# Background convolution of a gated-convolution and MLP kernel: products, fold and butterfly formed on VectorE instead of GpSimd

## The chip, the cores and the metric

The kernel runs on one core of one Trainium2 chip. The metric is the device time of one execution in microseconds. Before the change it is 2691.79 us, the median of three runs (2687.0 to 2693.62). The profile comes from one more execution, of 2694.62 us, whose instructions span 2692.4 us.

## The reference

Two layers, each of a gated long convolution A and an MLP B, act on x of 2048 tokens by 1024 channels, with residuals (layernorm without weights, written `ln`):

```
def _A_ref(q, k, v, shift_k, ssm_k, ssm_D):
    k_shift = sum over t < 4 of k_pad[:, t:t + S] * shift_k[:, 3 - t]
    kv = k_shift * v
    y = irfft(rfft(kv, 2 * S) * rfft(ssm_k, 2 * S))[:S]     # long causal convolution per channel
    return q * (y + kv * ssm_D)

def _B_ref(x, w1, b1, w2, b2):
    r = max(x @ w1 + b1, 0)
    return (r * r) @ w2 + b2

x = A_q
x = x + A(ln(x), A_k, A_v, ...);  x = x + B(ln(x), ...)
x = x + A(ln(x), A_k, A_v, ...);  x = x + B(ln(x), ...)
```

The convolved signal kv does not depend on x, so the result y of the long convolution is the same in both layers and is computed once.

## The kernel before, in words

All engines work from lists that are written out when the program is made; each engine takes its own list strictly in order. The 2048 tokens are cut into four blocks of 512 (`T`). The MLP of one block in one layer is a unit, and `ORDER` lists seven units (the last one takes two blocks together). TensorE multiplies in float32r with every operand split into a high and a low part, three matmuls for one (`mm3`, L351 to L354). A weight tile is loaded into `wr` (L1067, L1070), its high part is cast on ScalarE (`w_hi`, L1080) and its low part, weight minus high part, is formed on VectorE (`w_lo`, L1088; in a few phases on GpSimd). Tiles for three steps ahead are split before a step's matmuls. VectorE also forms the low part of the squared activations (L1565), and takes finished sums of the second matmul out of PSUM (L1685). So TensorE's next step waits for VectorE's list whenever that list is late.

The long convolution runs in the background of these units. Block 0 is done in a first stage of its own (`first_block`, with a planner). For blocks 1 to 3 (`sb`):

- `fwd_x` and `fwd_g` transform 256-token pieces of the signal and of the filter and store them in DRAM, in three versions of each, so that one complex product is made of three real ones (`PAIRS`). VectorE does most of their elementwise work (L382, L384, L424, L461, L481 to L501).
- `prod_stream` loads the transformed pieces into `cx` and `cg` (L642). For output piece j of a channel group and version it multiplies pieces 0 to j of one with pieces j to 0 of the other (`mult`, L542) and sums over the pieces (`red`, L546). Here j runs from 2 to 7. The product has 128 x (j + 1) elements per partition and is stored in `cp` (three buffers) with the j + 1 terms of one sum next to each other. The multiply itself walks through it term by term, so its reads are dense and its stores go in steps of j + 1 words, which is 3 to 8. The sum then reads `cp` densely.
- After the three versions of a group, `fin` combines them: a fold (L692, 512 elements), and a tick later a butterfly of an add and a subtract (L696, L697, 256 elements each). For block 1 plain matmuls follow, for blocks 2 and 3 a split into high and low part (L578 on VectorE) and matmuls for the way back.

`Later` puts a call a given number of ticks later in the program. A tick of `plag` passes with each product. Products are put between the matmul steps at a fixed rate per step (`pace`), slowly in the 18 steps at the end of a unit. The products of blocks 1 and 2 lie in units 0 to 2, those of block 3 in units 3 and 4 (the first few at the end of unit 2). After that there are none.

Before the change the product is on GpSimd, `red` is on VectorE two ticks later, and fold and butterfly are on GpSimd (`FIN` has a letter for each of the blocks 1 to 3: G is GpSimd, V is VectorE).

Of the kernel before, what the change touches and what calls it, by code (L numbers as in the profile page):

```python
# [44 lines left out]
NORM_0 = "VA"  # L45
AHEAD_0 = 4
BURST = 1.06
FIN = "GGG"
PACE_SLACK = {1: 74, 3: 10}
PACE_TO = {1: 2}  # L50
PLAIN = 1
# [196 lines left out]
def tile_h3_mlp(ctx: ExitStack, tc: tile.TileContext, q, kT, vT, shk, ssmT, ssmD, w1, b1, w2, b2,  # L248
                fwd_t, pro_t, inv_t, sgn_t, out):
    nc = tc.nc  # L250
    V, A, G, PE, SY = nc.vector, nc.scalar, nc.gpsimd, nc.tensor, nc.sync
# [284 lines left out]
    def prod_stream():  # L536
        lag = plag
        sums, inv = [0, 0], [0, 0]

        def mult(st, xt, gt, j):  # L540
            pr = cv.tile([P, CU, j + 1], F32, name="cp", bufs=3)
            G.tensor_mul(pr.rearrange("p c i -> p i c"), xt[:, 0:j + 1], gt[:, j::-1])  # L542
            st["pr"] = pr

        def red(st, sm, ty, jj):
# [2 lines left out]
        def fin(st, sm, sb, g, k):  # L548
            s = sm.rearrange("p k j c -> p k (j c)")
            E = ENG[FIN[sb - 1]]  # L550
            if k == 0:
# [81 lines left out]
        def load(n):  # L633
            sb, g, ty = units[n]
            nb = BT * sb + BT
            two = nb <= NBL // 2
            if n % 2 == 0 or not two:
                for nm in ("cx", "cg"):
                    share[nm] = cv.tile([P, 2 if two else 1, nb, CU], F32, name=nm, bufs=2)
            got[n] = [share[nm][:, n % 2 if two else 0] for nm in ("cx", "cg")]  # L640
            for t, src in zip(got[n], (XD[PAIRS[ty][0]], GD[PAIRS[ty][1]])):
                SY.dma_start(t, src[g, :, :nb])  # L642
            when[n] = lag.n

        def fill(n):
            sb = units[n][0]
            room = 3 if BT * sb + BT <= NBL // 2 and n % 2 else 2
            for m in range(n + 1, min(n + room + 1, len(units))):
                if m not in when:
                    if (units[m][0], units[m][1] // 2) not in fwd_done or (m > n + 2 and units[m][0] != sb):  # L650
                        return
                    load(m)

        pair = sm = None
        for n, (sb, g, ty) in enumerate(units):
            while n not in when:
                if (sb, g // 2) in fwd_done:
                    load(n)
                else:
                    lag.tick()  # L660
                    yield None
            while lag.n < when[n] + 2:
                lag.tick()
                yield None
            if ty == 0:
                while sums[0] - sums[1] >= 2:
                    lag.tick()
                    yield None
                sums[0] += 1
                sm = cv.tile([P, 3, BT, CU], F32, name="sm", bufs=2)  # L670
                if g % 2 == 0:
                    pair = {}
            for jj in range(BT):
                j = BT * sb + jj
                st = {"pair": pair}
                mult(st, *got[n], j)
                lag.at(2, red, st, sm, ty, jj)
                if jj == BT - 1:
                    if ty == 2:
                        lag.at(3, fin, st, sm, sb, g, 0)  # L680
                    fill(n)
                lag.tick()
                yield (j + 1) * CU * 1e-3
# [865 lines left out]
    lag = slag  # L1549
    xT = first_block()  # L1550
    pds = prod_stream()
    ml = shut.enter_context(tc.tile_pool(name="ml", bufs=1, reuse_waits="tile"))
    def relu2(st, k):
# [770 lines left out]
```

## Time and profile before

| | |
|---|---|
| median of three runs | 2691.79 us |
| profiled execution | 2694.62 us |
| its span | 2692.4 us |
| TensorE busy | 2629.6 us |
| VectorE busy | 2007.0 us |
| ScalarE busy | 1107.6 us |
| GpSimd busy | 1010.4 us |

The profile names the engines PE (TensorE matmuls), PEld (its weight loads), DVE (VectorE), ACT (ScalarE), POOL (GpSimd) and SP (the queue that issues DMAs). Rows name a source line, an operation, the tiles as output<-inputs, and the shape. "x81 | 76.4, 953 | 10.7" means 81 instructions, busy for 76.4 us together, 953 ns each on average, and 10.7 us in which the engine stood idle just ahead of them. A row of a table of windows gives a stretch of time, then the busy time and the count of each engine in it.

### The profile page before, as it was taken

How to read it: one execution, taken by the hardware profiler on the slowest of the kernel's cores; microseconds unless marked ns; L12 is line 12 of the kernel's file. 1: busy time of each engine (PE TensorE's matmuls, PEld its weight loads, DVE VectorE, ACT ScalarE, POOL GpSimd, SP SyncE). 2: the span in 40 equal slices, each digit the busy share in tenths (PEclk: the TensorE clock that was granted, in tenths of full speed). 3: DMA queues.
4: the chain of work that ended last, by engine and by line, in shares of the span. 5: the costliest groups of instructions: out<-in, count | busy, mean ns of one | idle time of the engine just before them, and what ended most of it. 6: DMA issues, size and time to landing. Idle time of an engine off the chain costs nothing.

```text
span 2692.4 us, 36210 instructions
## 1 busy us (share of the span) xinstructions
PE 2629.6 (98%) x12433; PEld 2204.0 (82%) x12433; DVE 2007.0 (75%) x2957; ACT 1107.6 (41%) x1890; POOL 1010.4 (38%) x641
## 2 busy tenths in 40 slices
PE   7999999899999999999999999999999999999999
PEld 6888787788888888888888888888788778888887
DVE  7878888779887878779767765456778787778553
ACT  3444344343434323343233422335444564444342
POOL 2436665156551744417454275000100006646111
PEclk9999999999999999999999999999999999999999
DMA  7799898679988999888987888689889886888653
GB/s 249 258 306 311 294 306 281 237 267 364 350 299 308 315 328 308 274 293 307 342 304 258 301 291 314 202 266 314 302 295 306 285 300 234 276 259 323 230 188 126
DMA packets 380840, 765.52 MB, mean 284 GB/s; under 512 B 44128, under 2 KB 159472, under 8 KB 377584
## 3 DMA queue, kind: packets, MB, share of 16 engines
q1 hardware_dynamic: 380656, 763.20, 82.7%
q8 instruction: 98, 1.61, 0.2%
q14 instruction: 86, 0.70, 0.1%
HBM read 585.85 MB, written 177.21 MB: 283 GB/s over the span
## 4 chain that ended last, share of the span: by engine, by line
PE 76%; DVE 8%; DMA 8%; POOL 2%; issue 2%; ACT 2%; SPq 1%; DVEq 0%; POOLq 0%; ACTq 0%
PE p L353 22%; PE p L352 22%; PE p L354 22%; PE pt L353 2%; PE pt L354 2%; PE pt L352 2%; PE p L1162 2%; DMA wr<-w 2%; DMA whl<-wd_m 1%; DVE whl L1088 1%; DMA cx<-xd 1%; DMA cg<-gd 1%; DVE st L713 1%; DMA yt<-yd 1%; POOL cp L542 1%
## 5 line engine op out<-in xcount | busy, mean ns | idle before, releaser
L542 POOL TENSOR_TENSOR cp<-cx,cg 128x384 f32<-128x384 f32 (+5 forms) x288 | 543.3, 1899 | 571.4 <-DVE sm L546 378.1
L352 PE MATMUL p<-xh,whl 128*128 128x512 f32 (+1 forms) x1504 | 577.7, 384 | 5.5 <-DMA whl<-wd_m 3.2
L354 PE MATMUL p<-xh,whl 128*128 128x512 f32 (+1 forms) x1504 | 573.5, 381 | 0.6 <-POOL whl L1088 0.6
L353 PE MATMUL p<-xl,whl 128*128 128x512 f32 (+1 forms) x1504 | 573.4, 381 | 0.1
L1080 ACT CAST whl<-wr 128x512 fp32r<-128x512 f32 x545 | 331.7, 619 | 477.1 <-PE p L354 270.6
L1088 DVE TENSOR_TENSOR whl<-wr,whl 128x512 fp32r<-128x512 f32 x495 | 427.5, 875 | 130.7 <-ACT whl L1080 130.1
L352 PE MATMUL p<-whl,rh 128*128 128x512 f32 x1204 | 476.0, 395 | 4.9 <-DMA whl<-wd_m 2.6
L353 PE MATMUL p<-whl,rh 128*128 128x512 f32 x1204 | 471.2, 391 | 4.8 <-DVE whl L1088 4.7
L354 PE MATMUL p<-whl,rl 128*128 128x512 f32 x1204 | 470.6, 391 | 0.0
L352 PEld LDWEIGHTS p<-xh,whl 128*128 128x128 f32 x1504 | 284.1, 189 | 60.9 <-issue 2.4
L354 PEld LDWEIGHTS p<-xh,whl 128*128 128x128 f32 x1504 | 283.6, 189 | 55.5 <-POOL whl L1088 0.8
L353 PEld LDWEIGHTS p<-xl,whl 128*128 128x128 f32 x1504 | 283.9, 189 | 52.4 <-DVE xl L1475 0.3
L1565 DVE TENSOR_TENSOR rl<-wr,rh 128x512 fp32r<-128x512 f32 x140 | 142.4, 1017 | 181.5 <-ACT rh L1562 181.1
L352 PEld LDWEIGHTS p<-whl,rh 128*128 128x128 f32 x1204 | 227.3, 189 | 53.8 <-DMA whl<-wd_m 5.2
L353 PEld LDWEIGHTS p<-whl,rh 128*128 128x128 f32 x1204 | 227.3, 189 | 51.5 <-DVE whl L1088 6.4
L354 PEld LDWEIGHTS p<-whl,rl 128*128 128x128 f32 x1204 | 227.1, 189 | 47.7
L546 DVE TENSOR_REDUCE sm<-cp 128x128 f32<-128x384 f32 (+5 forms) x288 | 249.5, 874 | 11.7 <-POOL cp L542 11.7
L1557 ACT ACTIVATE wr<-p,b1t 128x512 f32<-128x512 f32 x138 | 95.2, 690 | 369.8 <-PE p L354 367.2
L1088 POOL TENSOR_TENSOR whl<-wr,whl 128x512 fp32r<-128x512 f32 x50 | 71.5, 1431 | 274.1 <-ACT whl L1080 257.2
L1685 DVE TENSOR_TENSOR acc<-p,acc 128x512 f32<-128x512 f32 x152 | 99.8, 686 | 83.6 <-PE p L354 83.6
L1044 POOL TENSOR_TENSOR sr<-sr 128x512 f32<-128x512 f32 x14 | 19.9, 1420 | 341.3 <-DMA pd<-wr 303.8
L692 POOL TENSOR_TENSOR sm<-sm 128x512 f32<-128x512 f32 x48 | 69.1, 1440 | 131.5 <-DVE sm L546 123.8
(369 smaller groups left out, 4367.0 us busy)
## 6 DMA issues: line engine op xcount, KB each, us to landing
whl<-wd_m SPq DMA_DIRECT2D x323, 512.0 KB, 5.7
wr<-w SPq DMA_DIRECT2D x441, 256.0 KB, 5.6
wd_m<-whl SPq DMA_DIRECT2D x70, 512.0 KB, 6.4
wr<-td SPq DMA_DIRECT2D x112, 256.0 KB, 4.8
cx<-xd SPq DMA_DIRECT2D x48, 512.0 KB, 5.7
cg<-gd SPq DMA_DIRECT2D x48, 512.0 KB, 6.7
tq<-hd SPq DMA_DIRECT2D x24, 1024.0 KB, 7.4
gd<-fg SPq DMA_DIRECT2D x72, 256.0 KB, 5.9
```

Of the source, the lines that this page charges most:

```text
L352: PE.matmul(o, lh, rh, start=start, stop=False)
L353: PE.matmul(o, lh, rl, start=False, stop=False)
L354: PE.matmul(o, ll, rh, start=False, stop=stop)
L542: G.tensor_mul(pr.rearrange("p c i -> p i c"), xt[:, 0:j + 1], gt[:, j::-1])
L546: V.tensor_reduce(sm[:, ty, jj], st["pr"], axis=AX.X, op=OP.add)
L692: E.tensor_add(s[:, 1:3], s[:, 1:3], s[:, 0:1].to_broadcast([P, 2, s.shape[2]]))
L1080: A.copy(t[:, 0], raws[n]["t"])
L1088: ENG[e[n % len(e)]].tensor_sub(t[:, 1], raws[n]["t"], t[:, 0].bitcast(F32))
L1162: PE.matmul(o, lh, r, start=start, stop=stop)
L1557: A.activation(r, st["o"], AF.Relu, bias=b1t[:, st["f"]:st["f"] + 1])
L1565: V.tensor_sub(st["lo"], st["r"]["t"], st["hi"].bitcast(F32))
L1685: V.tensor_add(accs[tt][:, d], o, accs[tt][:, d])
```

## The change

Products, fold and butterfly go to VectorE for all three blocks, and a sum stands one tick behind its product instead of two. Since the tick passes right after the product has been issued, nothing but the steps of `fin` can come between.

```
-FIN = "GGG"
+FIN = "VVV"
...
-            G.tensor_mul(pr.rearrange("p c i -> p i c"), xt[:, 0:j + 1], gt[:, j::-1])
+            V.tensor_mul(pr.rearrange("p c i -> p i c"), xt[:, 0:j + 1], gt[:, j::-1])
...
-                lag.at(2, red, st, sm, ty, jj)
+                lag.at(1, red, st, sm, ty, jj)
```

The lists of TensorE, ScalarE and the DMA queue keep their order; only buffer numbers differ. The piece below is VectorE's list where the first products of block 1 stand, in unit 0; `whl` is a weight tile whose low part is made, `cp` a product, `sm` the sums.

```order
 L1088 TENSOR_TENSOR whl<-wr,whl 128x512
-L546 TENSOR_REDUCE sm<-cp 128x128
-L1088 TENSOR_TENSOR whl<-wr,whl 128x512
-L546 TENSOR_REDUCE sm<-cp 128x128
+L542 TENSOR_TENSOR cp<-cx,cg 128x3x128
+L546 TENSOR_REDUCE sm<-cp 128x128
+L542 TENSOR_TENSOR cp<-cx,cg 128x4x128
+L546 TENSOR_REDUCE sm<-cp 128x128
+L1088 TENSOR_TENSOR whl<-wr,whl 128x512
 L419 TENSOR_TENSOR fy<-pt,fx 128x8x64
```

Where two sums stood around a weight split, two products with their sums now stand in one piece ahead of it. The next piece is VectorE's list before, in a stretch of unit 3 with products of block 3 (7 and 8 pieces); `rl` is the low part of an activation.

```order
L1565 TENSOR_TENSOR rl<-wr,rh 128x512
L546 TENSOR_REDUCE sm<-cp 128x128
L1088 TENSOR_TENSOR whl<-wr,whl 128x512
L1565 TENSOR_TENSOR rl<-wr,rh 128x512
L546 TENSOR_REDUCE sm<-cp 128x128
L1088 TENSOR_TENSOR whl<-wr,whl 128x512
L546 TENSOR_REDUCE sm<-cp 128x128 x2
L578 TENSOR_TENSOR yl<-sm,yh 128x4x64 x2
```

And this is the same stretch of VectorE's list after the change.

```order
L1565 TENSOR_TENSOR rl<-wr,rh 128x512
L542 TENSOR_TENSOR cp<-cx,cg 128x8x128
L692 TENSOR_TENSOR sm<-sm 128x512
L546 TENSOR_REDUCE sm<-cp 128x128
L1088 TENSOR_TENSOR whl<-wr,whl 128x512
L1565 TENSOR_TENSOR rl<-wr,rh 128x512
L542 TENSOR_TENSOR cp<-cx,cg 128x7x128
L696 TENSOR_TENSOR sm<-sm 128x256
L697 TENSOR_TENSOR sm<-sm 128x4x64
L546 TENSOR_REDUCE sm<-cp 128x128
L1088 TENSOR_TENSOR whl<-wr,whl 128x512
```

A product stands ahead of each sum, and the fold and the butterfly, where they fall due, stand between a product and its sum. GpSimd's list loses all of these and keeps its few weight splits and its residual adds.

## The prediction

> **What bounds the kernel now.** I read the page first.
>
> ```profile
> span 2692.4 us, 36210 instructions
> PE 2629.6 (98%) x12433; PEld 2204.0 (82%) x12433; DVE 2007.0 (75%) x2957; ACT 1107.6 (41%) x1890; POOL 1010.4 (38%) x641
> ```
>
> TensorE is busy for all but 62.8 us of the span, so the kernel is bound by it, and a change on other engines can save those 62.8 us at most. It can cost more, if VectorE becomes too slow for TensorE. A mean of 75% doesn't say whether it does; that is read by stretches. Five stretches hold most of the products: block 1 in unit 0, block 2 in units 1 and 2, block 3 in units 3 and 4. The windows show first what each engine does there, then GpSimd's products alone; the last row is the one in which VectorE is fullest.
>
> ```profile
> core 0: us, PE busy (x) PEld busy (x) DVE busy (x) ACT busy (x) POOL busy (x), PEclk, DMA share, GB/s
> 202.00:471.00 269.00, 255.48 (x1187) 213.70 (x1186) 232.02 (x330) 114.25 (x208) 162.75 (x130) 0.98 0.90 298
> 606.00:807.00 201.00, 199.39 (x948) 167.44 (x947) 179.33 (x230) 82.74 (x150) 114.28 (x70) 1.00 0.96 338
> 875.00:1144.00 269.00, 268.84 (x1281) 226.31 (x1280) 213.64 (x265) 92.40 (x168) 144.93 (x84) 1.00 0.90 306
> 1211.00:1346.00 135.00, 135.00 (x640) 113.52 (x639) 113.51 (x133) 43.20 (x78) 82.68 (x41) 1.00 0.91 325
> 1548.00:1682.00 134.00, 134.00 (x604) 111.42 (x603) 81.27 (x86) 32.72 (x57) 84.94 (x45) 1.00 0.84 302
> ...
> 202.00:471.00 269.00, 117.38 (x87) 0.98 0.90 298
> 606.00:807.00 201.00, 88.37 (x46) 1.00 0.96 338
> 875.00:1144.00 269.00, 105.19 (x53) 1.00 0.90 306
> 1211.00:1346.00 135.00, 58.18 (x25) 1.00 0.91 325
> 1548.00:1682.00 134.00, 61.40 (x27) 1.00 0.84 302
> ...
> 605.00:673.00 68.00, 66.39 (x311) 55.27 (x310) 65.80 (x88) 25.66 (x46) 42.58 (x26) 1.00 1.01 361
> ```
>
> I call them A to E. VectorE has 37, 22, 55, 21 and 53 us left in them. GpSimd's products alone take 117, 88, 105, 58 and 61. They must shrink a lot to fit.
>
> **What the change takes off VectorE.** VectorE's busy time holds more than work. Two DVE rows and one POOL row of the timeline:
>
> ```profile
> 738.76 0.68 DVE L1565 TENSOR_TENSOR rl<-wr,rh 128x512 fp32r<-128x512 f32 x1
> 739.36 2.33 DVE L1088 TENSOR_TENSOR whl<-wr,whl 128x512 fp32r<-128x512 f32 x1
> ...
> 738.91 2.24 POOL L542 TENSOR_TENSOR cp<-cx,cg 128x768 f32<-128x768 f32 x1 [2.89 <-DVE sm L546]
> ```
>
> The first subtract started ahead of GpSimd's product and took 0.68 us. The second, of the same size, started under it, and ended 0.54 us after it (741.69 against 741.15): it stood still while GpSimd worked. How much that is shows against rows from 1750 to 2150 us, where GpSimd does next to nothing:
>
> ```profile
> L1088 DVE TENSOR_TENSOR whl<-wr,whl 128x512 fp32r<-128x512 f32 x131 | 86.7, 685 | 10.1 <-ACT whl L1080 9.6
> L1565 DVE TENSOR_TENSOR rl<-wr,rh 128x512 fp32r<-128x512 f32 x6 | 4.2, 693 | 16.9 <-ACT rh L1562 16.9
> L787 DVE SCALAR_TENSOR_TENSOR px<-yt,rs,px 128x512 f32<-128x512 f32 x8 | 6.0, 752 | 0.3
> L1642 DVE TENSOR_TENSOR cp<-yh,cx 128x1024 fp32r<-128x1024 f32 x7 | 8.6, 1222 | 1.0 <-ACT cx L1638 1.0
> ```
>
> Here are the same kinds in A, and then in D:
>
> ```profile
> L1088 DVE TENSOR_TENSOR whl<-wr,whl 128x512 fp32r<-128x512 f32 x81 | 76.4, 953 | 10.7 <-ACT whl L1080 10.6
> L382 DVE SCALAR_TENSOR_TENSOR fx<-fx,shkt 128x512 f32<-128x512 f32 x21 | 22.1, 1051 | 0.5
> L1565 DVE TENSOR_TENSOR rl<-wr,rh 128x512 fp32r<-128x512 f32 x21 | 18.6, 885 | 5.3 <-ACT rh L1562 5.0
> ...
> L1088 DVE TENSOR_TENSOR whl<-wr,whl 128x512 fp32r<-128x512 f32 x11 | 16.0, 1458 | 0.0
> L1565 DVE TENSOR_TENSOR rl<-wr,rh 128x512 fp32r<-128x512 f32 x13 | 13.6, 1047 | 10.4 <-ACT rh L1562 10.4
> L578 DVE TENSOR_TENSOR yl<-sm,yh 128x256 fp32r<-128x256 f32 x8 | 11.0, 1420 | 0.0
> L382 DVE SCALAR_TENSOR_TENSOR fx<-fx,shkt 128x512 f32<-128x512 f32 x6 | 9.5, 1582 | 0.1
> ```
>
> In A the blocked time is 81 x 0.268 + 21 x 0.299 + 21 x 0.192 = 32 us, or 0.20 us for each of GpSimd's 163 us. In D it is 11 x 0.773 + 13 x 0.354 + 8 x 1.0 (a dense 256 takes 0.42, below) + 6 x 0.83 = 26 us, 0.31 for each of 83. Smaller rows come on top in A, so I take 0.28 per us of GpSimd's moved work.
>
> **What it puts on VectorE.** The rows of 685 and 1222 ns give a dense two-input operation 148 ns + 1.05 ns per element (256 elements: 417 ns). The moved operations on GpSimd, over the whole run:
>
> ```profile
> L542 POOL TENSOR_TENSOR cp<-cx,cg 128x1024 f32<-128x1024 f32 x48 | 124.3, 2589 | 133.6 <-DVE sm L546 133.5
> L542 POOL TENSOR_TENSOR cp<-cx,cg 128x384 f32<-128x384 f32 x48 | 59.8, 1246 | 75.2 <-DMA cg<-gd 72.2 <-DVE sm L546 3.0
> L692 POOL TENSOR_TENSOR sm<-sm 128x512 f32<-128x512 f32 x48 | 69.1, 1440 | 131.5 <-DVE sm L546 123.8 <-DMA whl<-wd_m 4.3 <-ACT whl L1080 3.4
> L696 POOL TENSOR_TENSOR sm<-sm 128x256 f32<-128x256 f32 x49 | 46.7, 954 | 4.6 <-DVE sm L692 3.9
> L697 POOL TENSOR_TENSOR sm<-sm 128x256 f32<-128x256 f32 x49 | 42.7, 871 | 3.8
> ```
>
> A product costs GpSimd 440 ns + 2.10 ns per element. Fold and butterfly come once in six products and cost it 3.27 us; their stores are in long runs, so on VectorE they cost 0.68 + 2 x 0.42, less an overlap that the next rows show.
>
> ```profile
> 1766.16 0.68 DVE L1088 TENSOR_TENSOR whl<-wr,whl 128x512 fp32r<-128x512 f32 x1
> 1766.76 0.42 DVE L1599 TENSOR_TENSOR cx<-cx 128x256 f32<-128x256 f32 x1
> 1767.22 0.42 DVE L1600 TENSOR_TENSOR cx<-cx 128x256 f32<-128x256 f32 x1
> ```
>
> An independent operation starts 0.08 us before the last one ends (0.60 after its start of 0.68). One that reads what the last one wrote starts 0.04 us after it. A set of fold and butterfly is thus 0.60 + 2 x 0.34 = 1.28 us. A sum directly behind its product waits, so a product occupies its whole duration and 0.04 more.
>
> The products' own price is the unknown. No VectorE row of this trace stores elements in steps of several words, as L542 does. From below the dense row bounds it: 0.183 us + 1.05 ns per element. From above there is GpSimd's row with these very stores, 2.10 ns per element, though GpSimd may be held up by something else. I take the second rate, since its store pattern is the one that moves: 0.183 us + 2.10 ns, or GpSimd's time less 0.26 us for each product.
>
> [...]
>
> | us | A | B | C | D | E |
> |---|---|---|---|---|---|
> | VectorE before | 232 | 179 | 214 | 114 | 81 |
> | blocked time gone (0.28 x moved GpSimd time) | -46 | -32 | -38 | -20 | -21 |
> | fold, butterfly (products / 6 x 1.28) | +18 | +10 | +12 | +5 | +5 |
> | products, dense stores | +56 | +43 | +51 | +28 | +30 |
> | or products at 2.10 ns | +95 | +76 | +91 | +52 | +54 |
> | VectorE after, dense | 260 | 200 | 239 | 127 | 95 |
> | VectorE after, 2.10 ns | 299 | 234 | 279 | 151 | 120 |
> | length before | 269 | 201 | 269 | 135 | 134 |
>
> (Each column is rounded after its sum.) The dense products are half of what is left when 0.44 us each is taken off GpSimd's time, plus 0.183 us each. VectorE can be filled to 65.8 of 68 us, 0.97, with TensorE nearly full beside it (last window row). Then A needs 299 / 0.97 = 308 us, +39; B 241, +40; C 288, +19; D 155, +20; E fits. Together +118 us. No store of products can move to a quieter place, for their steps are fixed in the program, and after 1690 us there are none. Between the stretches, at the ends of units, products are few.
>
> Two smaller edits. The sum one tick earlier costs only the 0.12 us of start that I have counted. And VectorE now waits itself for the loads of `cx` and `cg`, with weight splits (L1088) and TensorE's matmuls (L352 to L354) queued behind it:
>
> ```profile
> POOL cp L542 <- DMA cg<-gd: 182.0, 43, 14.4
> ...
> DVE sm L546 <- POOL cp L542: 11.7, 16, 1.9
> ```
>
> GpSimd waits 182 us for these loads because it runs ahead. The sums, two ticks on, waited only 11.7 us for load and product together, so I take nothing here, and 12 us or so at worst.
>
> The profiled execution gives 2694.6 + 118 = 2813 us; the median of the runs lies 2.8 us lower, so I predict **2810 us**.
>
> **The rivals.**
>
> *Stores that cost VectorE nothing.* Then only B overflows: 200 / 0.97 = 206, +6 us, 2698 us at the median, which a measurement of this kernel hardly tells from before (0.3% is 8 us). For it speaks that GpSimd's rate may be its reading of two inputs and not its stores; against it, that steps are untested on VectorE. Fuller short windows within a stretch could make it some 20 us more. Chance 0.18.
>
> *Stores that cost VectorE more than GpSimd.* At a fifth more per element A to D need 324, 255, 304 and 165 us and E still fits: +175 us, 2867 us. GpSimd's slow pace would then have hidden a slower store. It decides as soon as the elements cost over 2.3 ns. Chance 0.18. [...]
>
> *Faster, as single long blocks did the harm.* TensorE's worst wait for VectorE in A is for one of its transform steps:
>
> ```profile
> PE pt L437 <- DVE fx L384: 9.2, 3, 6.7
> ```
>
> If such waits came from single blocks of over 2 us and not from load, TensorE's 13.5 idle us of A go: 2694.6 - 13.5 - 2.8 = 2678 us. It decides if A's load on VectorE falls, so if a product of 448 elements (A's mean) costs under (46 - 18) / 87 = 0.32 us; the dense row makes it 0.65. Chance 0.07.
>
> That the change doesn't do what it says is ruled out by the lists: none of these operations is left on GpSimd.
>
> **How the numbers follow.** The forecast, a price between 1.5 and 2.3 ns, has 0.55; the rivals 0.18, 0.18 and 0.07; 0.02 is left, on the slow side, for the wait on loads. Faster is 0.07, within 0.3% is 0.10 (over half of the dense case), slower 0.83. The range goes from the lower dense case, 2700, past the fifth more (2867) to 2890 for fuller short windows. It leaves out the faster case, half of the dense one and a little above.
>
> **What would show it.** Right: L542 on DVE at about 0.95 us for 384 elements and 2.3 for 1024; L1088 back at 685 ns in A to D; DVE near 97% there, with PE idle and its waits going to DVE `whl` L1088; E and all after 1690 us as before. Wrong: L542 at 0.55 and 1.22 us (the dense case); DVE idle while PE waits, or waits of L542 for DMA over 12 us; blocks that go on under GpSimd's few other operations.

## The result and the profile after

The kernel after takes 2759.08 us (median of four runs, 2755.32 to 2759.68) against 2692.66 for the kernel before in the same comparison: a ratio of 1.0248, 95% interval 1.023 to 1.0266. It is 66 us slower. The profiled execution took 2758.96 us with a span of 2757.2. The page of the kernel after:

```profile
span 2757.2 us, 36003 instructions
PE 2650.6 (96%) x12433; PEld 2209.9 (80%) x12433; DVE 2256.1 (82%) x3389; ACT 1107.2 (40%) x1890; POOL 319.8 (12%) x209
```

TensorE stands idle for 106.6 us instead of 62.8, and its matmuls take 21 us more. VectorE has 249 us more of busy time.

Part of the 21 us is the clock. These are matmuls of the kernel after behind a gap in which TensorE waited for a weight split, then the window of the 3.4 us that follow; the last three figures of that row are the granted clock, the DMA share and GB/s.

```profile
653.65 0.39 PE L353 MATMUL p<-xl,whl 128*128 128x512 f32 x1
656.21 0.69 PE L354 MATMUL p<-xh,whl 128*128 128x512 f32 x1 [2.17 <-DVE whl L1088]
656.70 0.63 PE L352 MATMUL p<-xh,whl 128*128 128x512 f32 x1
...
656.40:659.80 3.40, 3.40 (x9) 2.66 (x9) 3.33 (x8) 0.00 (x0) 0.00 (x0) 0.51 0.73 217
```

The gap lasts 2.17 us, and for 3.4 us from there the clock is at half and a matmul takes 0.63 us instead of 0.39. The clock records of the two traces hold more of this after the change: 51 us at half clock ahead of the last instructions, against 34 us before, so some 9 us of the 66 are a slower clock (an estimate: half of the difference). In the kernel after, each of these stretches lies at a gap of TensorE of 1.1 us or more, and starts at most 2.2 us behind its end.

TensorE's list is the same instruction by instruction, so the same matmul can be found in both traces. How far it starts behind its place in the profiled execution of before shows where the time goes. The columns are the stretch in the trace of before, the lag at its end, and what the stretch added (at 202 us the lag was -2.2 us).

```
from-to of before     lag at the end   added   forecast
202-471   (A)              21.5        +23.7     +39
471-606                    23.4         +1.9
606-807   (B)              39.2        +15.8     +40
807-875                    41.8         +2.6
875-1144  (C)              48.6         +6.8     +19
1144-1211                  48.8         +0.3
1211-1346 (D)              56.8         +8.0     +20
1346-1548                  61.9         +5.1
1548-1682 (E)              64.0         +2.1       0
1682-2100                  63.9         -0.1       0
```

The loss sits in the stretches of the forecast, A most, and nothing is added once the products have ended. But every part is smaller than forecast. The windows of the kernel after over the same five stretches of work (A to E), and below them the products alone:

```profile
core 0: us, PE busy (x) PEld busy (x) DVE busy (x) ACT busy (x) POOL busy (x), PEclk, DMA share, GB/s
200.00:492.50 292.50, 263.08 (x1185) 217.32 (x1184) 278.83 (x460) 112.56 (x207) 0.00 (x0) 0.96 0.84 273
629.50:846.00 216.50, 204.65 (x947) 169.01 (x946) 211.01 (x298) 81.40 (x147) 0.00 (x0) 0.98 0.90 309
917.00:1192.50 275.50, 271.07 (x1279) 226.86 (x1278) 258.78 (x345) 92.47 (x167) 11.70 (x4) 0.99 0.88 302
1260.00:1403.00 143.00, 137.98 (x640) 114.36 (x639) 138.64 (x164) 43.51 (x78) 12.71 (x4) 0.99 0.88 308
1610.00:1746.00 136.00, 134.48 (x604) 111.22 (x603) 122.59 (x127) 32.99 (x57) 11.95 (x4) 1.00 0.83 310
...
200.00:492.50 292.50, 75.69 (x87) 0.96 0.84 273
629.50:846.00 216.50, 67.66 (x45) 0.98 0.90 309
917.00:1192.50 275.50, 86.88 (x53) 0.99 0.88 302
1260.00:1403.00 143.00, 50.34 (x24) 0.99 0.88 308
1610.00:1746.00 136.00, 53.27 (x26) 1.00 0.83 310
```

VectorE is now full in A, B and D (95, 97 and 97% of the longer stretch) and TensorE has gaps. What TensorE waits for in A, first in the kernel before, then in the kernel after:

```profile
PE p L353 <- DVE whl L1088: 0.2, 1, 0.2
```

```profile
PE p L353 <- DVE whl L1088: 7.1, 4, 2.5
PE p L354 <- DVE whl L1088: 3.8, 1, 3.8
```

The groups of the kernel after on VectorE, over the whole run, give the price of a product by size, and the old rows without GpSimd's blocking:

```profile
L542 DVE TENSOR_TENSOR cp<-cx,cg 128x384 f32<-128x384 f32 x48 | 32.4, 674 | 0.4 <-DMA cg<-gd 0.4
L542 DVE TENSOR_TENSOR cp<-cx,cg 128x512 f32<-128x512 f32 x48 | 51.4, 1071 | 0.0
L542 DVE TENSOR_TENSOR cp<-cx,cg 128x768 f32<-128x768 f32 x48 | 77.0, 1604 | 0.0
L542 DVE TENSOR_TENSOR cp<-cx,cg 128x1024 f32<-128x1024 f32 x48 | 104.6, 2180 | 0.0
L1088 DVE TENSOR_TENSOR whl<-wr,whl 128x512 fp32r<-128x512 f32 x495 | 357.6, 733 | 110.5 <-ACT whl L1080 107.4 <-DMA wr<-td 2.0 <-ACT sd L721 0.3
L578 DVE TENSOR_TENSOR yl<-sm,yh 128x256 fp32r<-128x256 f32 x64 | 26.6, 460 | 0.0
```

Less the fixed 148 ns, a product costs 1.37 ns per element with stores in steps of 3 words, 1.80 with 4, 1.90 with 6 and 1.98 with 8. With 5 and 7 words (1446 and 1932 ns) it is 2.03 and 1.99. The groups at 5, 7 and 8 words each hold one product of 3.6 to 4.3 us that stood still under GpSimd's residual adds; without it they come to 1.94 to 1.96. The forecast was 2.10 for all. L578 fell from 1088 to 460 ns and L1088 from 875 to 733. In A, where GpSimd now does nothing, L1088 takes 684 ns (953 before), as the prediction asked; in D, where a few residual adds remain, 777.

One view changed that the prediction didn't look at: what the DMA queue waits for. First the kernel before, then the kernel after (us in total, times, longest).

```profile
SPq L1076 <- PE p L354: 486.1, 200, 12.4
...
SPq L642 <- POOL cp L542: 59.6, 30, 5.6
```

```profile
SPq L642 <- DVE cp L542: 385.5, 91, 14.0
SPq L1076 <- PE p L354: 276.8, 130, 11.5
```

L642 loads `cx` and `cg` into one of two buffers each, and waits until the product that read the buffer is done. GpSimd ran ahead with its products and itself waited 182.0 us for the loads; VectorE doesn't run ahead and waits 4.4 us for them. Behind those loads in the queue stand the reloads of weights (L1076), and TensorE waits for them. Again the kernel before and the kernel after:

```profile
PE p L352 <- DMA whl<-wd_m: 5.8, 9, 1.6
```

```profile
PE p L352 <- DMA whl<-wd_m: 20.3, 22, 2.9
PE p L353 <- DVE whl L1088: 13.3, 8, 3.1
PE p L437 <- DVE fx L1201: 12.0, 3, 9.7
PE pt L437 <- DVE fx L384: 8.8, 3, 3.8
```

### The profile page after: what moved, and what is told of

Same layout as the page of the kernel before. It is cut to its first block, busy times and chain, and to the rows that moved or that the text cites. A ratio compares the mean times of both kernels' runs of the same rounds, so it can differ in the third digit from the quotient of the medians.

```text
span 2757.2 us, 36003 instructions
## 1 busy us (share of the span) xinstructions
PE 2650.6 (96%) x12433; PEld 2209.9 (80%) x12433; DVE 2256.1 (82%) x3389; ACT 1107.2 (40%) x1890; POOL 319.8 (12%) x209
## 4 chain that ended last, share of the span: by engine, by line
PE 42%; DVE 7%; DMA 5%; issue 2%; ACT 1%; POOL 1%; SPq 1%; DVEq 0%; POOLq 0%; ACTq 0%
PE p L352 12%; PE p L353 12%; PE p L354 12%; DMA whl<-wd_m 2%; PE pt L353 1%; PE pt L354 1%; PE pt L352 1%; DVE cp L542 1%; DMA wr<-w 1%; DVE whl L1088 1%; DVE st L713 1%; DMA sr<-w 1%; DMA px<-x 1%; DVE sm L546 0%; DMA x<-acc 0%
## 5 line engine op out<-in xcount | busy, mean ns | idle before, releaser
L1088 DVE TENSOR_TENSOR whl<-wr,whl 128x512 fp32r<-128x512 f32 x495 | 357.6, 733 | 110.5 <-ACT whl L1080 107.4
L542 DVE TENSOR_TENSOR cp<-cx,cg 128x384 f32<-128x384 f32 (+5 forms) x288 | 427.6, 1485 | 4.4 <-DMA cg<-gd 4.4
L1565 DVE TENSOR_TENSOR rl<-wr,rh 128x512 fp32r<-128x512 f32 x140 | 110.6, 790 | 85.6 <-ACT rh L1562 85.5
L1802 POOL TENSOR_TENSOR acc<-acc,px 128x1024 f32<-128x1024 f32 x20 | 58.2, 2938 | 1032.3 <-DMA px<-b 658.7
L1088 POOL TENSOR_TENSOR whl<-wr,whl 128x512 fp32r<-128x512 f32 x50 | 71.8, 1437 | 585.5 <-DMA wd_m<-whl 328.3
L354 PE MATMUL p<-whl,tq 128*128 128x512 f32 x276 | 107.5, 389 | 0.0
```

The source lines that it names most:

```text
L354: PE.matmul(o, ll, rh, start=False, stop=stop)
L542: V.tensor_mul(pr.rearrange("p c i -> p i c"), xt[:, 0:j + 1], gt[:, j::-1])
L1088: ENG[e[n % len(e)]].tensor_sub(t[:, 1], raws[n]["t"], t[:, 0].bitcast(F32))
L1565: V.tensor_sub(st["lo"], st["r"]["t"], st["hi"].bitcast(F32))
L1802: G.tensor_add(a, a, st["t"])
```

## The experiments

The main theory was that the stepped stores of the products fill VectorE (the store theory). The rivals: that product and sum stand as one piece in VectorE's list (lump), that the loads' waits in the DMA queue do it (queue), and that fold and butterfly do. When dense stores left a rest, the store theory was widened to the fullness theory: VectorE's work by stretch, of whatever kind, sets the loss.

### Dense stores

```
-            V.tensor_mul(pr.rearrange("p c i -> p i c"), xt[:, 0:j + 1], gt[:, j::-1])
+            V.tensor_mul(pr.rearrange("p c i -> p (c i)").rearrange("p (i c) -> p i c", c=CU),
+                         xt[:, 0:j + 1], gt[:, j::-1])
```

> The products stay on VectorE in the same order, but are stored one after the other without gaps, so each sum adds the wrong terms; nothing else differs. Store theory (the stepped stores of the product fill VectorE): the product falls from 0.67, 1.07, 1.40, 1.61, 1.88 and 2.13 us to 0.55, 0.68, 0.82, 0.95, 1.09 and 1.22, some 160 us less for VectorE, whose load in the first stretch (unit 0) falls from 279 to about 259 us; the time comes back to 2695 us, give or take 12. Lump theory (what costs is that product and sum stand as one dependent piece in VectorE's list ahead of the weight splits, whatever the store): the pieces stay, and the time stays over 2735.

2715.76 us, ratio 1.0097 (1.0082 to 1.0112): 43 us less than the kernel after. Groups of this run:

```profile
L542 DVE TENSOR_TENSOR cp<-cx,cg 128x1024 f32<-128x1024 f32 x48 | 60.5, 1261 | 0.0
L542 DVE TENSOR_TENSOR cp<-cx,cg 128x384 f32<-128x384 f32 x48 | 26.5, 552 | 0.0
```

The products cost about what the dense rows said, and about two thirds of the loss goes. The lump theory is out as the main cause. But the time stayed 9 us above the upper end of what the store theory expected: some 25 us of the loss are not the stores.

### Dense stores, summed by a tree of adds

```
-            pr = cv.tile([P, CU, j + 1], F32, name="cp", bufs=3)
-            V.tensor_mul(pr.rearrange("p c i -> p i c"), xt[:, 0:j + 1], gt[:, j::-1])
+            pr = cv.tile([P, j + 1, CU], F32, name="cp", bufs=3)
+            V.tensor_mul(pr, xt[:, 0:j + 1], gt[:, j::-1])
...
-            V.tensor_reduce(sm[:, ty, jj], st["pr"], axis=AX.X, op=OP.add)
+            pr = st["pr"]
+            n = pr.shape[1]
+            while n > 1:
+                h = n // 2
+                o = sm[:, ty, jj] if n == 2 else pr[:, 0:h] if h > 1 else pr[:, 0]
+                if h > 1:
+                    V.tensor_add(o, pr[:, 0:h], pr[:, n - h:n])
+                else:
+                    V.tensor_add(o, pr[:, 0], pr[:, n - 1])
+                n -= h
```

> Dense products stored piece after piece, summed by two or three dependent adds of halves instead of one sum: all on VectorE, with the reference's result. The adds of 8 pieces take 896 elements in three operations, about 1.37 us against 1.13 for the sum, so VectorE does some 40 us more than with dense stores alone. Store theory: 2705 us, between 2690 and 2720. Lump theory: more dependent operations in each piece, so slower than the changed kernel, over 2760.

2720.6 us, ratio 1.0117 (1.0101 to 1.0132). That is just above the upper end of the store theory. With 480 more operations on VectorE than in the kernel after, many of them dependent, the run is still 38 us shorter, against the lump theory.

### Stepped reads in place of stepped stores

```
-            pr = cv.tile([P, CU, j + 1], F32, name="cp", bufs=3)
-            V.tensor_mul(pr.rearrange("p c i -> p i c"), xt[:, 0:j + 1], gt[:, j::-1])
+            pr = cv.tile([P, j + 1, CU], F32, name="cp", bufs=3)
+            V.tensor_mul(pr, xt[:, 0:j + 1], gt[:, j::-1])
...
-            V.tensor_reduce(sm[:, ty, jj], st["pr"], axis=AX.X, op=OP.add)
+            V.tensor_reduce(sm[:, ty, jj], st["pr"].rearrange("p i c -> p c i"), axis=AX.X, op=OP.add)
```

> Dense products stored piece after piece, and one sum that reads with steps of 128 words: the step is moved from the store to a read. If a stepped read costs VectorE what a stepped store does (1.9 ns per element), the sum of 1024 elements goes from 1.21 to about 2.1 us and the time stays near 2755 us. If only stores are slow, the sums stay at 0.54 to 1.21 us and the time is that of dense stores, about 2695. The lump theory expects over 2735 either way.

2745.06 us, ratio 1.0204 (1.0189 to 1.022): 10 us under the expected 2755, and far from 2695. The sums of this run:

```profile
L546 DVE TENSOR_REDUCE sm<-cp 128x128 f32<-128x1024 f32 x48 | 95.7, 1994 | 1.1
...
L546 DVE TENSOR_REDUCE sm<-cp 128x128 f32<-128x512 f32 x48 | 51.5, 1073 | 1.4
L546 DVE TENSOR_REDUCE sm<-cp 128x128 f32<-128x384 f32 x48 | 28.6, 596 | 1.9
```

A stepped read costs much the same as a stepped store, 1.80 ns per element less the fixed 148 ns, so the layout's price moves from one operation to the other. Sums over three pieces are the exception, at 1.17. Nothing here says why.

### All stores in steps of 8 words

```
-            pr = cv.tile([P, CU, j + 1], F32, name="cp", bufs=3)
+            pr = cv.tile([P, CU, 8], F32, name="cp", bufs=3)[:, :, 0:j + 1]
```

> All products are stored with steps of 8 words, whatever the number of pieces; the work is the same. Store theory, with a price by the step: the product of 384 elements goes from 0.67 to about 0.89 us and that of 512 from 1.07 to 1.14, so VectorE has 13 us more in the first stretch and the time rises by about that, to 2771 us; 640 to 1024 elements stay. If the price went by the number of elements and not by the step, no row moves and the time stays at 2759.

2768.49 us, ratio 1.0292 (1.0275 to 1.031), 9 us over the kernel after. The two rows that had smaller steps:

```profile
L542 DVE TENSOR_TENSOR cp<-cx,cg 128x512 f32<-128x512 f32 x48 | 54.3, 1131 | 0.0
...
L542 DVE TENSOR_TENSOR cp<-cx,cg 128x384 f32<-128x384 f32 x48 | 42.9, 895 | 1.6 <-DMA cg<-gd 1.6
```

The price goes by the step: 384 elements cost 895 ns with steps of 8 and 674 with steps of 3.

### Three buffers for the loads

```
-                    share[nm] = cv.tile([P, 2 if two else 1, nb, CU], F32, name=nm, bufs=2)
+                    share[nm] = cv.tile([P, 2 if two else 1, nb, CU], F32, name=nm, bufs=3)
...
-            pr = cv.tile([P, CU, j + 1], F32, name="cp", bufs=3)
+            pr = cv.tile([P, CU, j + 1], F32, name="cp", bufs=1)
```

Other stages that borrow `cx`, `cg` and `cp` take the same seven buffers under their new names.

> The changed kernel with three buffers instead of two for each of the loads cx and cg (and one cp instead of three, which a product followed by its own sum doesn't miss). Queue theory (a part of the loss comes through the DMA queue: the loads L642 wait 385.5 us for a product on VectorE to free their buffer, against 59.6 before, and the weight reloads L1076 stand behind them): the waits of L642 fall under 100 us, TensorE's waits for reloaded weights from 20 to about 6 us, and the time falls by 10 to 25 us, to 2734 to 2749. If only VectorE's fullness counts, the queue's waits fall too, but the time stays within 5 us of 2759.

2744.92 us, ratio 1.0193 (1.0178 to 1.0208): 14 us less than the kernel after, with VectorE as busy as there (2252 us). The queue and TensorE in this run:

```profile
SPq L642 <- DVE cp L542: 19.8, 12, 6.1
...
PE p L352 <- DMA whl<-wd_m: 5.1, 9, 1.0
```

The waits go as the queue theory said: TensorE's fall by 15 us and the run by 14. This cost is real, and smaller than that of the stores.

### Tree and three buffers

The two edits above together.

> Dense products with the tree of adds, and three buffers for the loads. The dense kernels left 25 to 30 us over the kernel before. Queue theory: most of that goes, 2695 to 2708 us. If the rest is VectorE's fullness or the pieces in its list, it stays at 2721, give or take 5.

2714.06 us, ratio 1.0076 (1.0057 to 1.0095): 6.5 us less than the tree alone, short of the 13 that were expected at least. With the tree the queue was a smaller part of the rest: TensorE's waits for reloaded weights fell from 10.3 to 6.3 us.

### Fold and butterfly alone back on GpSimd

```
-FIN = "VVV"
+FIN = "GGG"
```

> Products on VectorE as in the changed kernel, fold and butterfly back on GpSimd. VectorE loses 48 x 1.28 = 61 us of work and stands still again under 157 us of GpSimd's (0.28 of that is 44), so 17 us less for it. Store theory: little moves, 2745 to 2762 us. If fold and butterfly on VectorE were a main cost, the time would fall under 2730.

2766.99 us, ratio 1.0278 (1.0258 to 1.0297). That is 8 us more than the kernel after, 5 over the range. Fold and butterfly are no main cost beside the products. Taking them off VectorE left its busy time at 2252 us against 2256, though it has some 61 us less of work. That comes back in two ways. Operations stand still again under GpSimd: L1088 went from 733 to 765 ns, L1565 from 790 to 829, L382 from 762 to 841, and all products from 428 to 442 us, which is 41 us together. And fold and butterfly no longer stand between a product and its sum: 244 sums instead of 172 now wait for the product directly ahead of them. At the 0.21 us of a wait that the run with two ticks shows below, that is some 15 us.

### Only fold and butterfly on VectorE

```
-            V.tensor_mul(pr.rearrange("p c i -> p i c"), xt[:, 0:j + 1], gt[:, j::-1])
+            G.tensor_mul(pr.rearrange("p c i -> p i c"), xt[:, 0:j + 1], gt[:, j::-1])
...
-                lag.at(1, red, st, sm, ty, jj)
+                lag.at(2, red, st, sm, ty, jj)
```

> Only fold and butterfly on VectorE; products on GpSimd and sums two ticks later, as in the kernel before. VectorE gets 61 us of work and loses about 44 us of standing still. Store theory: 2690 to 2702 us, the change's loss is in the products. If fold and butterfly on VectorE were a main cost: over 2715.

2705.05 us, ratio 1.0042 (1.0025 to 1.0059), 3 us over the range, and 10 under 2715. VectorE's busy time rose by 87 us, not by 17. The reason stands in the groups of this run:

```profile
L578 DVE TENSOR_TENSOR yl<-sm,yh 128x256 fp32r<-128x256 f32 x64 | 69.2, 1121 | 0.0
...
L697 DVE TENSOR_TENSOR sm<-sm 128x256 f32<-128x256 f32 x49 | 58.6, 1197 | 1.7
L692 DVE TENSOR_TENSOR sm<-sm 128x512 f32<-128x512 f32 x50 | 50.7, 1015 | 0.4
```

With the products still on GpSimd, the moved steps stand still under them: the subtract takes 1197 ns here and 425 in the kernel after. L578 is as slow as in the kernel before (1088 ns). So the move of this half kept the blocking of the other half.

### The sum two ticks behind

```
-                lag.at(1, red, st, sm, ty, jj)
+                lag.at(2, red, st, sm, ty, jj)
```

> The changed kernel with the sum two ticks behind its product, as before the change, so that another product stands between them on VectorE. A sum directly behind its product starts 0.12 us later than behind an independent operation; some 200 of the 288 sums stand so, 24 us of VectorE's time. Fullness theory (VectorE's work by stretch sets the loss): 5 to 15 us less than the changed kernel's 2759, so 2744 to 2754. Lump theory: the dependent pieces are the main cost, so under 2735.

2732.2 us, ratio 1.0154 (1.0138 to 1.0171): 27 us less than the kernel after, nearly twice what the fullness theory allowed for, and under the lump theory's bound by 3. The list tells more than the bound. In this kernel 235 of 288 sums still stand directly behind a product (180 in the kernel after), only it is another product than their own. So the pieces are still there; what went is the wait of a sum for its own product. Rows of the kernel after show that wait, and the last one an operation that needn't wait; below them are two rows of this run:

```profile
1302.15 2.15 DVE L542 TENSOR_TENSOR cp<-cx,cg 128x1024 f32<-128x1024 f32 x1
1304.34 1.22 DVE L546 TENSOR_REDUCE sm<-cp 128x128 f32<-128x1024 f32 x1
1305.47 1.89 DVE L542 TENSOR_TENSOR cp<-cx,cg 128x896 f32<-128x896 f32 x1
1307.18 0.76 DVE L578 TENSOR_TENSOR yl<-sm,yh 128x256 fp32r<-128x256 f32 x2
```

```profile
1306.96 1.88 DVE L542 TENSOR_TENSOR cp<-cx,cg 128x896 f32<-128x896 f32 x1
1308.67 1.20 DVE L546 TENSOR_REDUCE sm<-cp 128x128 f32<-128x1024 f32 x1
```

In the kernel after the sum starts 0.04 us after its product's end. But L578, which doesn't need the product ahead of it, starts 0.18 us ahead of that product's end, and so does the sum of this run (0.17). In the kernel after 172 sums start late, in this run none: its 235 sums behind a product start 0.17 us ahead of the product's end on average. Behind a stepped product a wait thus costs 0.21 us on average and not the 0.12 of the expectation, and 172 x 0.21 = 36 us of VectorE's time. Its busy time is 39 us less, and 27 us of the run go with it. The half of the lump theory that speaks of dependence holds, then, at this size. The sums' places in the list changed too, and no run parts that from the wait. With dense stores an independent operation starts only 0.08 us ahead of the product's end, and a wait costs 0.12 us.

### Dense stores and three buffers

The first edit and the buffers together.

> Dense stores (each sum adds the wrong terms) and three buffers for the loads: no stepped store, no tree, no wait of the queue. The tree lost 6.5 us with the third buffer (2721 to 2714). Fullness theory: 2704 to 2712 us, and what is left over the kernel before comes from about 130 us more of work on VectorE. If the queue were the rest of the loss: 2697 or less.

2702.82 us, ratio 1.0042 (1.0029 to 1.0055): 13 us less than with dense stores alone and 1 below the range, so the queue's part shows here as with stepped stores. TensorE's waits for reloaded weights fell from 16.6 to 5.4 us. Some 12 us over the kernel before are left.

### And without fold and butterfly

```
-                fold(E, s)
+                None
...
-                st["z"] = butterfly(E, s)
+                st["z"] = parts(s)
```

Here `parts` gives the same views as the butterfly and works nothing; the edit is made at both calls.

> As the one with dense stores and three buffers, but fold and butterfly are left out (so the convolution's result is not formed rightly): 61 us less on VectorE. Fullness theory: another 8 to 15 us less, 2692 to 2702 us. If the rest is the product standing in front of its sum and the weight split, nothing moves.

2685.49 us, ratio 0.9984 (0.9974 to 0.9993): 17 us less than the last one, and 7 below the expected range. The rest of the loss goes with the 56 us that VectorE is less busy, while products still stand in front of their sums and the splits. The steps left out also no longer stand between products and sums, and what follows no longer waits for them; the run doesn't part that from their work.

### Tree, and two ticks

```
-                lag.at(1, red, st, sm, ty, jj)
+                lag.at(2, red, st, sm, ty, jj)
```

> Dense products with the tree of adds (2721 us with the tree directly behind its product), now two ticks behind. The first add no longer waits for its own product; the second and third still depend on the one ahead. Bubble theory (each operation that reads what the last one wrote starts 0.12 us later; the sum two ticks on won 27 us with stepped stores, where VectorE was fuller): 10 to 20 us less, 2701 to 2711 us, and the best of the versions with products on VectorE and the reference's result, though still not under the kernel before. If the sum's place in the list mattered only together with the stepped stores: 2716 to 2724.

2714.39 us, ratio 1.009 (1.0073 to 1.0107): 6 us less than the tree, which lies between the two expectations. With dense products a wait is worth 0.12 us and not 0.21, and VectorE is less full; which of the two makes the tick worth 6 us here and 27 with stepped stores isn't parted.

No version that does the whole computation with products on VectorE beat the kernel before. The best are two with the tree, at 2714 us.

## Why the prediction was right

It forecast slower, 2810 us with a range of 2700 to 2890; measured were 2759. Direction, place and mechanism hold, and the size is 66 us instead of 118. With the loads that VectorE really had in A to D, the forecast's own rule (load / 0.97 less the length before) gives 18, 17, 0 and 8 us, together 43. The other 23 us lie where it forecast nothing or less: 10 between the stretches, 7 in C, 5 in A, 2 in E. So two terms came out too slow, others were missing, and the errors cancelled in part; that the total was no further off is partly luck.

- **VectorE becomes the bound in A to D: right.** It fills 94 to 97% there, TensorE's waits for `whl` L1088 in A went from 0.2 to 10.9 us, E adds 2 us, and nothing is added after it. Across the runs the time rises with VectorE's busy time, but not by it alone. The runs "only products" (fold and butterfly back on GpSimd) and "3 buffers" are equally busy and 22 us apart, and with fold and butterfly left out VectorE is 43 us busier than before and the run some 4 us shorter. The medians are from several comparisons, in which the kernel before took 2690 to 2693 us:

```
run                          VectorE busy us   median us
before                           2007.0         2691.8
dense, 3 buffers, no fold        2050.3         2685.5
only fold and butterfly          2094.4         2705.1
dense, 3 buffers                 2106.2         2702.8
dense                            2106.7         2715.8
tree, two ticks                  2133.4         2714.4
tree                             2144.0         2720.6
tree, 3 buffers                  2145.4         2714.1
two ticks                        2217.3         2732.2
stepped reads                    2242.6         2745.1
only products                    2251.9         2767.0
3 buffers                        2252.2         2744.9
after                            2256.1         2759.1
steps of 8                       2267.5         2768.5
```

- **The products' price: right in kind, too high in size.** The forecast took GpSimd's 2.10 ns per element; VectorE takes 1.37 to 1.96 when it doesn't stand still. In A, B, C and D its products took 76, 68, 87 and 50 us, where 95, 76, 91 and 52 were forecast. The largest miss is A, with the small steps.
- **The blocked time that goes: too small.** Put together from the rows (load before, plus products, plus fold and butterfly, minus load after), it was 47, 46, 54, 30 and 17 us in A to E, where 46, 32, 38, 20 and 21 were forecast. By this reckoning the factor of 0.28 should have been 0.35 (194 us for 560 us of moved work); all that the other terms have wrong is in it. These two terms make VectorE's load in B 211 us and not 234, in C 259 and not 279. Two small slips stand beside it. The subtract of a butterfly starts 0.03 us behind the end of its add in all 49 sets, so a set costs some 0.12 us more than the 1.28 of three that overlap. And by the table's own rule fold and butterfly in C and E come to +11 and +6, not +12 and +5.
- **The fill of 0.97: right where VectorE is the bound**, with 0.95, 0.97 and 0.97 in A, B and D.
- **"I take nothing here" for the loads: half right.** VectorE's own wait for them is 4.4 us. The prediction asked who waits for the loads and not whom the loads wait for. Their buffers come free later, and the weight reloads behind them in the DMA queue cost 14 us with stepped stores and 13 with dense ones. With three buffers C adds 2.6 us instead of 6.8 and B 12.5 instead of 15.8. A adds 29 instead of 24, so the gain lies outside A, where the kernel after has no wait for a reloaded weight.
- **The sum directly behind its product** was in the forecast's sum, which counts a product's whole duration and 0.04 us. But what the earlier tick costs was put too low. The 0.12 us come from rows behind dense operations; behind a stepped product it is 0.21 us, or 36 us of VectorE's time for 172 sums. The run with two ticks puts it at 27 us of the run; it is no small edit as the prediction called it.
- **The clock had no term.** The longer gaps of TensorE brought more time at half clock, some 9 us of the 66 by the estimate above. No run shows it apart from the gaps.
- **The rival of long blocks** fell: the longest wait of L437 for L384 went from 6.7 to 3.8 us, and A still grew by 24. The rival of a dearer store fell too: no run shows its fifth more per element as a price of the stores, and the dearest group of products in the kernel after costs 2.03 ns per element, where that rival needed over 2.3.
- **The dense rival** was about right in its own case. Dense stores alone come to 2716 us, where 2698 and some 20 more for short windows stood; with the third buffer it is 2703.

The parts are not a sum. Dense stores took away 43 us, two ticks 27, the third buffer 14, which is 84 of 66. The first two overlap, as both take time off a full VectorE and a wait behind a dense product is shorter: with the tree, the two ticks took 6. The third buffer took 14 with stepped stores, 13 with dense ones and 6.5 with the tree.

## What to carry to other kernels

When an operation changes its engine, price its access pattern on the new engine. GpSimd, at 2.1 ns per element, hid a stepped store: its stepped product of 512 elements took 1519 ns and its fold of 512 elements 1440. On VectorE the stepped product of that size takes 1071 ns and the dense one 682. Count on both sides, what the move adds to the new engine and what it stops blocking there, by stretches and not by the mean. And look up in the DMA queue's own waits which loads wait for the moved instruction to free a buffer, and what stands behind them.

## What the runs showed of the hardware that was not expected

- Stores in steps of words cost VectorE, per float32 element beyond 148 ns fixed, 1.05 ns dense, 1.37 at 3 words, 1.80 at 4, and 1.90 to 1.96 at 5 to 8. Reads of a sum in steps of 128 words cost 1.80 over 4 or 8 pieces, but 1.17 over 3.
- An operation that doesn't need the product ahead of it starts 0.17 us ahead of the product's end where the stores are stepped, 0.08 us where they are dense. One that needs it starts 0.04 us after the end in both. So a wait costs 0.21 us in one case and 0.12 in the other.
- Moving fold and butterfly alone raised VectorE's busy time by 87 us for 61 us of work. With products on VectorE, moving them as well left it within 4 us (2251.9 to 2256.1) and made the run 8 us shorter.
